# The first sequence's two channel mixing chunks side by side, and the weight conversions spread evenly over attention

## The chip, the cores and the metric

The kernel runs on one core of a Trainium2 chip. The metric is device microseconds of one execution; before the change the median of three runs is 427.49 us (426.55 to 429.01). The profiled execution is one of these runs, and all durations below come from it.

TensorE (PE) multiplies, with its weight loads (PEld) beside it; VectorE (DVE), ScalarE (ACT) and GpSimd (POOL) work on tiles; SP issues nearly all DMAs. Each engine executes its own queue in order.

## The reference, cut to what matters

Three layers follow each other: a linear attention with decay (2 sequences, 8 heads, 768 tokens, head size 48), a mixer, and a mixture of 8 experts in which each token takes one.

```python
# attention, per head:  y_t = r_t (S + u k_t v_t);  S = w S + k_t v_t
# mixer, per sequence, x is [768, 384]:
h  = np.maximum(xt @ w_tok1, 0.0) @ w_tok2        # over tokens, 768 -> 256 -> 768
u  = x + h.transpose(0, 2, 1)
h2 = np.maximum(u @ w_ch1, 0.0) @ w_ch2           # over channels, 384 -> 1536 -> 384
x  = u + h2
# experts: logits and a gate choose e per token
h = np.maximum(x[b, s] @ w1[e], 0.0);  out[b, s] = p[e] * (h @ w2[e])
```

The four mixer weights arrive as float64, everything else as float32.

## The kernel before, in words

Every product of the mixer is done in float32 by three matmuls: both operands are split into a rounded part (hi) and a rest (lo), and hi·hi, lo·hi, hi·lo are added in PSUM (`mm3`, L353). A split is a copy on ACT and a subtraction on DVE or POOL.

**Conversions.** The float64 weights are converted on the chip in 16 items, each half of a weight block: `c1k` and `c2k` are blocks of the channel mixing's first and second product, `t1` and `t2` are the token mixing's. One item takes the absolute value on ACT (`conv_abs`, L294), three DVE parts (`conv_parts`, L314: part A is two instructions, L320 and L321, part B is L325, part C is L327), and then a copy on ACT and a subtraction on POOL (`conv_finish`, L284), which are issued when the next item begins. Part C also issues the load of a later item's raw bits. `conv_do(n)` issues n parts at the place where it is called. The order of all instructions is the order in which the Python code issues them; no scheduler changes it.

**Attention** is a loop over 12 tiles of 128 tokens (t = 0 to 11, six per sequence). Iteration t does for tile t+1 the scores on PE and the masks `am` on DVE, for tile t+2 the scaling of `rk` (`pre_rk`, L369) and the product `pp` on DVE, then the state update, the values `y` of tile t on PE, the `bon` products of tile t+1 on ACT (L391), and `finish(t)` (L479), which forms `x` on DVE, issues a conditional DMA into it (taken only where the decay lies outside a range) and splits `x` into `xh` and `xl`. Transposes (`turn`, and `pre_ks`, which makes `kt` of tile t+2) and the token mixing's products (`mix1`, `mix2`) close the iteration. `CONV_T`, `CONV_N` and the other tables at the top say at which t how many parts are issued: three parts in each of t = 2 to 6 and 8 to 10, two ahead of `finish` and one behind it.

**The tail and the channel mixing.** Behind the loop stand the rest of the token mixing and the first steps of the channel mixing, with two more items among them (`CONV_B`). The channel mixing has four chunks n of 384 tokens, two per sequence, and each runs 12 steps f (`chan_step`, L676). A step is nine matmuls `ch1` into a PSUM tile `c1`, the split of its rectified result into `hh` (ACT) and `hl` (DVE) and, two steps later, nine matmuls `ch2` into three accumulators. The chunks run one after another. Steps f use quarter-blocks in order, so chunk 0 needs two new items for every two steps; the last six items are issued among its steps, one whole item per step. While chunk n+1 runs, chunk n's tokens are routed to experts (`route`, whose `yield`s cut it into ten pieces, two per step from f = 3). `usplit(n)` splits chunk n's input into `uh` and `ul`.

PSUM has eight banks: three accumulators (`acc0` to `acc2`) and five that all other tiles take in turn (`ps_tile`).

Of the kernel before, what the change touches and what calls it, by code (L numbers as in the profile page):

```python
# [30 lines left out]
T1 = 4  # L31
CONV_T = (2, 3, 4, 5, 6, 8, 9, 10)
CONV_B = (1, 1, 1, 1, 1, 1, 0, -1, 0, 0)
ABS_NEXT = (10, 11, 12, 13, 14)
ABS_B = (0, 3)
CONV_N = (0, 0, 2, 2, 2, 2, 2, 2, 2, 2, 2, 0)
HI_MIN, HI_MAX = (float(x) for x in np.array([0x38100000, 0x47EFFFFF], np.int32).view(np.float32))
# [40 lines left out]
def _emit(ctx, tc, a_in, wu, u_row, wt1, wt2, wc1, wc2, wgl, wex, cst_in, cst_a, out):  # L78
# [24 lines left out]

    psw = ctx.enter_context(tc.tile_pool(name="psw", bufs=5, space=PSUM))
    psa = ctx.enter_context(tc.tile_pool(name="psa", bufs=1, space=PSUM))
# [28 lines left out]
    def load_a(t, part=None):  # L134
        if t not in a_t:
            rk = ap.tile([128, 1024], F32, tag="rk", name=f"rk{t}", bufs=4)
            v = ap.tile([128, DM], F32, tag="v", name=f"v{t}", bufs=3)
# [117 lines left out]
    conv = []  # L255
    for k in range(6):
        for h in range(2):
            conv.append((k, h))
    conv += [(k, h) for h in range(2) for k in (6, 7)]
    conv_raw, conv_pend, cpool_, wb2 = [], [], [], []  # L260
    nload = [0]

    def conv_load():
        n = nload[0]
        if n >= len(conv) or (n >= 12 and not cpool_):
# [6 lines left out]
        if n < 12:  # L272
            raw = rawp.tile([128, 768, 2], I32, tag="raw", name="raw")
        else:
            raw = cpool_[0].tile([128, 768, 2], I32, tag=f"e{n - 12}", name="raw")
# [17 lines left out]
    def conv_abs(n):  # L293
# [7 lines left out]
        if wb2:  # L301
            if n < 12:
                late[n % 2] = cpool_[0].tile([128, 1536], I32, tag=f"raw{6 + n % 2}", name="f")
# [10 lines left out]
    def conv_parts():  # L314
        for n in range(len(conv)):
# [19 lines left out]
    tail_at = [-1]  # L335

    def conv_tail(n):
        tail_at[0] += 1
        for j in range(2):
            if ABS_B[j] == tail_at[0]:  # L340
                conv_abs(8 + j)
        if n < 0:
            conv_finish()
        else:
            conv_do(n)
# [174 lines left out]
    def mix2(b, half, c, k=2):  # L520
        w2h, w2l = W["t2"]
        ps = acc_tile(k)
        for m in range(2):
# [9 lines left out]
    def usplit(n):  # L533
        b, half = divmod(n, 2)
        for c in range(3):
            u = xT[b][:, c, half * 384:(half + 1) * 384]
            hi = hp.tile([128, 384], F32R, tag=f"uh{c}", name="uh", bufs=1)
            lo = hp.tile([128, 384], F32R, tag=f"ul{c}", name="ul", bufs=1)
            nc.scalar.copy(hi, u)
            nc.vector.tensor_tensor(out=lo, in0=u, in1=hi.bitcast(F32), op=ALU.subtract)  # L540
            uhl[c] = (hi, lo)

# [25 lines left out]
    for t in range(NT):  # L568
        if t + 3 < NT:
            load_a(t + 3, 0)  # L570
        if t < 2:
            conv_load()
# [30 lines left out]
        if t >= 7:  # L603
# [34 lines left out]

    def ch1(f):
        ch, cl = W[f"c1{f // 4}"]  # L640
        ps = ps_tile("c1", (128, 384))
        for c in range(3):
            o = f % 4 // 2 * 768 + c * 256 + f % 2 * 128
            mm3(ps, ch[:, o:o + 128], cl[:, o:o + 128], *uhl[c], c == 0, c == 2)
        return ps
# [21 lines left out]

    later = []
# [20 lines left out]

    def chan(n, side, then, start=0):  # L690
        for f in range(start, 12):
            chan_step(n, f, side, then)
        for _ in side:
            pass

    conv_tail(CONV_B[0])
    turn(11)
    chan_step(0, 0, nothing, None)
    conv_tail(CONV_B[1])
    mix1(11)  # L700
    conv_tail(CONV_B[2])
    chan_step(0, 1, nothing, None)
    conv_tail(CONV_B[3])
    for half in range(2):
        for c in range(3):
            mix2(1, half, c, (2, 0, 1)[c])
            conv_tail(CONV_B[4 + 3 * half + c])
# [10 lines left out]
    for _ in range(4):  # L718
        conv_load()
# [648 lines left out]
```

## Time and profile before

| what | value |
|---|---|
| median of 3 runs | 427.49 us |
| the profiled execution | 426.55 us |
| its span, first to last instruction | 425.0 us |
| PE busy in the span | 399.2 us (94%) |
| DVE busy | 278.5 us (66%) |
| ACT busy | 192.7 us (45%) |
| POOL busy | 90.0 us (21%) |

The shares are means over stages that differ. Until about 102 us the kernel is in attention, until 117 us in the tail, until 154 us in chunk 0, and chunks 1 to 3 end near 275 us; then the experts follow. The waits say what ended the idle time of an engine, and a group of rows with a shape such as 128x768 names partitions and elements. "Clock" is the share of full speed granted to TensorE.

### The profile page before, as it was taken

Reading aid. Unit: us, or ns where it says so; the run is one execution under the profiler, and the core shown is the slowest. Engines: PE = TensorE matmul, PEld = TensorE weight load, DVE = VectorE, ACT = ScalarE, POOL = GpSimd, SP = SyncE. Lnnn points to the kernel's source line nnn. Section 1 sums busy time; section 2 is a strip of 40 time slices with the busy share of each in tenths; the row PEclk is TensorE's granted clock in tenths of the full one; section 3 lists DMA queues with packets and bytes.
Section 4 is the critical chain, followed back from the end, with each engine's and each line's share of the span. In section 5 each row is a group of like instructions: output and inputs, shape, how many; then the busy total and the mean of one; then the engine's idle time right before and its main releaser. Section 6 shows DMA issues by size and latency. Waiting matters only on the chain. (4 is left out here: it accounts for less than half of the span.)

```text
span 425.0 us, 8637 instructions
## 1 busy us (share of the span) xinstructions
PE 399.2 (94%) x3348; PEld 379.3 (89%) x3348; DVE 278.5 (66%) x592; ACT 192.7 (45%) x459; POOL 90.0 (21%) x83
## 2 busy tenths in 40 slices
PE   7997699997899699999999999999999999999994
PEld 3687597986799599999999999999999999999994
DVE  6669998987979944624361447659677676675431
ACT  2587468683443342112311221642755666654531
POOL 2013444145233310000000001131261132111110
PEclk9898999998999999999999999999999999999998
DMA  7364475323390000100100010881779867662000
GB/s 260 129 210 144 148 256 180 122 89 113 99 349 36 1 2 10 48 0 2 56 2 0 2 56 13 323 300 55 259 285 403 283 220 229 211 209 102 11 31 14
DMA packets 18336, 55.88 MB, mean 131 GB/s; under 512 B 3921, under 2 KB 7795, under 8 KB 18290
## 3 DMA queue, kind: packets, MB, share of 16 engines
q1 hardware_dynamic: 16370, 49.96, 33.9%
q0 software_dynamic: 1920, 5.32, 4.0%
q8 instruction: 27, 0.44, 0.4%
q14 instruction: 19, 0.16, 0.1%
HBM read 52.31 MB, written 5.91 MB: 137 GB/s over the span
## 5 line engine op out<-in xcount | busy, mean ns | idle before, releaser
L1030 DVE TENSOR_TENSOR we<-wr,we 128x768 fp32r<-128x768 f32 x54 | 51.6, 960 | 14.8 <-ACT we L1029 14.8
L359 ACT ACTIVATE hh<-c 128x384 fp32r<-128x384 f32 x48 | 23.4, 490 | 74.4 <-PE c L356 65.7
L360 DVE SCALAR_TENSOR_TENSOR hl<-c,hh 128x384 fp32r<-128x384 f32 x48 | 26.4, 552 | 43.3 <-ACT hh L359 43.3
L356 PE MATMUL acc<-hl,c 128*128 128x384 f32 x144 | 48.6, 337 | 3.5 <-DVE hl L360 3.5
L359 ACT ACTIVATE hh<-e 128x256 fp32r<-128x256 f32 (+1 forms) x72 | 25.2, 350 | 57.3 <-PE e L356 43.4
L360 DVE SCALAR_TENSOR_TENSOR hl<-e,hh 128x256 fp32r<-128x256 f32 (+1 forms) x72 | 27.2, 378 | 35.2 <-ACT hh L359 35.1
L354 PE MATMUL acc<-hh,c 128*128 128x384 f32 x144 | 49.7, 345 | 0.0
L355 PE MATMUL c<-uh,c 128*128 128x384 f32 x144 | 48.5, 337 | 0.6 <-POOL c L288 0.6
L354 PE MATMUL c<-uh,c 128*128 128x384 f32 x144 | 48.5, 337 | 0.0
L356 PE MATMUL c<-ul,c 128*128 128x384 f32 x144 | 48.4, 336 | 0.0
L355 PE MATMUL acc<-hh,c 128*128 128x384 f32 x144 | 48.3, 335 | 0.0
L1029 ACT CAST we<-wr 128x768 fp32r<-128x768 f32 x56 | 46.0, 829 | 2.8 <-DMA wr<-in_wex 2.8
L354 PE MATMUL acc<-we,hh 128*128 128x384 f32 x120 | 42.6, 355 | 0.0
L355 PE MATMUL acc<-we,hl 128*128 128x384 f32 x120 | 40.3, 336 | 0.0
L356 PE MATMUL acc<-we,hh 128*128 128x384 f32 x120 | 40.2, 335 | 0.0
L288 POOL TENSOR_TENSOR c<-f,c 128x768 fp32r<-128x768 f32 x12 | 24.4, 2029 | 45.0 <-ACT c L287 45.0
L356 PEld LDWEIGHTS acc<-hl,c 128*128 128x128 f32 x144 | 27.0, 188 | 4.4 <-DVE hl L360 4.4
L355 PEld LDWEIGHTS c<-uh,c 128*128 128x128 f32 x144 | 27.2, 189 | 1.2 <-POOL c L288 1.2
L354 PEld LDWEIGHTS c<-uh,c 128*128 128x128 f32 x144 | 27.3, 190 | 0.0
L354 PE MATMUL e<-gx,we 128*128 128x256 f32 x96 | 27.3, 284 | 0.0
L356 PEld LDWEIGHTS c<-ul,c 128*128 128x128 f32 x144 | 27.2, 189 | 0.0
L355 PEld LDWEIGHTS acc<-hh,c 128*128 128x128 f32 x144 | 27.1, 188 | 0.0
(228 smaller groups left out, 948.1 us busy)
## 6 DMA issues: line engine op xcount, KB each, us to landing
wr<-in_wex SPq DMA_DIRECT2D x32, 768.0 KB, 7.2
raw<-in_wc SPq DMA_DIRECT2D x12, 768.0 KB, 5.3
rk<-in_a_in SPq DMA_DIRECT2D x12, 512.0 KB, 5.7
raw<-in_wt SPq DMA_DIRECT2D x4, 768.0 KB
v<-in_a_in SPq DMA_DIRECT2D x12, 192.0 KB
x<-yscr SPq DMA_DIRECT2D x12, 192.0 KB
xs<-rows SPq DMA_DIRECT2D x8, 192.0 KB
xs<-row SPq DMA_DIRECT2D x4, 192.0 KB, 3.6
```

Source lines behind the costliest of these rows:

```text
L288: nc.gpsimd.tensor_tensor(out=ls, in0=f, in1=hs.bitcast(F32), op=ALU.subtract)
L354: nc.tensor.matmul(ps, lhsT=lh, rhs=rh, start=first, stop=False)
L355: nc.tensor.matmul(ps, lhsT=ll, rhs=rh, start=False, stop=False)
L356: nc.tensor.matmul(ps, lhsT=lh, rhs=rl, start=False, stop=last)
L359: nc.scalar.activation(out=hi, in_=ps, func=ACTF.Relu)
L360: nc.vector.scalar_tensor_tensor(out=lo, in0=ps, scalar=0.0, in1=hi.bitcast(F32), op0=ALU.max, op1=ALU.subtract)
L1029: nc.scalar.copy(hi[:, cs], raw[:, cs])
L1030: eng.tensor_tensor(out=lo[:, cs], in0=raw[:, cs], in1=hi[:, cs].bitcast(F32), op=ALU.subtract)
```

## The change

1. Chunks 0 and 1 run their steps alternately: chunk 0 does f = 0 to 2 in the tail, then (1,0), (1,1), and then (0,f), (1,f-1) for f = 3 to 11, and (1,11). Eight items are issued among these 21 steps, one part and two parts in turn.
2. For that, chunk 0's accumulators take three of the five shared banks (tags w2 to w4), and the `c1` tiles use the two others (`turn_of`); chunk 1's split input gets tiles of its own, in memory that attention used (`ue`), and is split at the end of the tail.
3. The routing of both chunks moves to chunk 2's steps, with two or three pieces per step from f = 0.
4. In attention two parts are issued in each of t = 1 to 10, all ahead of `finish`, and one at t = 11. The first item's absolute value is taken at t = 0, each later one when the part C ahead of it is issued. One item (three parts) stands in the tail. Items alternate c1 and c2 blocks.
5. `pre_ks(t+2)` moves from the end of iteration t to a place right behind `pre_rk(t+2)`, ahead of the state update and the values. `finish`'s conditional DMA moves from SP to ACT, `v` gets a fourth buffer, and both first raw loads are issued at t = 0.
6. The last `mix2` calls of each sequence use shared banks instead of the accumulators.

```diff
-CONV_T = (2, 3, 4, 5, 6, 8, 9, 10)
-CONV_B = (1, 1, 1, 1, 1, 1, 0, -1, 0, 0)
...
-CONV_N = (0, 0, 2, 2, 2, 2, 2, 2, 2, 2, 2, 0)
+CONV_N = (0, 2, 2, 2, 2, 2, 2, 2, 2, 2, 2, 1)
+CONV_B = (0, 1, 0, 0, 0, 1, 1, -1, 0, 0)
...
+    turn_of, nps = [0, 1, 2, 3, 4], [0]
+
+    def ps_tile(name, shape=(128, 512), k=None):
+        if k is None:
+            k = turn_of[nps[0] % len(turn_of)]
+            nps[0] += 1
+        return psw.tile(list(shape), F32, tag=f"w{k}", name=name)
...
-            if n in ABS_NEXT:
+            if n < len(conv) - 1 and (n < 7 or wb2):
                 conv_abs(n + 1)
...
-        nc.sync.dma_start(out=x, in_=yscr[t], cond=bad > 0, cond_hint=False)
+        nc.scalar.dma_start(out=x, in_=yscr[t], cond=bad > 0, cond_hint=False)
...
         if t + 2 < NT:
             pre_rk(t + 2)
+            if (t + 2) % NCH < NCH - 1:
+                pre_ks(t + 2)
...
-        if t in CONV_T:
-            conv_abs(CONV_T.index(t))
         values(t)
...
-        if t in CONV_T:
+        if t < NT - 1:
             conv_do(CONV_N[t])
-        else:
-            conv_finish()
         finish(t)
-        if t in CONV_T:
-            conv_do(3 - CONV_N[t])
...
-            ch_acc[n] = [acc_tile(c) for c in range(3)]
+            if n == 0:
+                turn_of[:] = [0, 1]
+            ch_acc[n] = [acc_tile(c) if n else ps_tile("acc", (128, 384), 2 + c) for c in range(3)]
...
-    chan_step(0, 1, nothing, None)
+    chan_step(0, 1)
+    chan_step(0, 2)
...
-    conv_abs(10)
+    conv_abs(8)
+    usplit(1)
...
-    later.extend([conv_do] * 10)
-    chan(0, nothing, lambda: usplit(1), 2)
-    chan(1, route(0, None), lambda: usplit(2))
-    chan(2, route(1, None), lambda: usplit(3))
-    chan(3, first(), lambda: None)
+    later.extend([lambda j=j: conv_do(1 + j % 2) for j in range(16)])
+    later.append(conv_do)
+    order = [(1, 0), (1, 1)]
+    for f in range(3, 12):
+        order += [(0, f), (1, f - 1)]
+    order.append((1, 11))
+    side = itertools.chain(route(0, None), route(1, None))
+    done0 = order.index((0, 11))
+    for j, (n, f) in enumerate(order):
+        chan_step(n, f, side, 2 if j >= done0 + 3 else 0)
+    for f in range(12):
+        chan_step(2, f, side, 2 + (f % 3 == 2))
+    for f in range(12):
+        if f == 3:
+            side = itertools.chain(side, first())
+        chan_step(3, f, side, 2)
```

DVE's queue in chunk 0 before: between two rows `hl`, each the split of one step, stands one whole item.

```order
L360 SCALAR_TENSOR_TENSOR hl_1841<-c1_1830,hh_1840 128x384
L320 TENSOR_SCALAR f_1750<-f_1750 128x768
L321 TENSOR_SCALAR f_1750<-f_1750 128x768
L325 SCALAR_TENSOR_TENSOR f_1750<-raw_1754,f_1750 128x768
L327 SCALAR_TENSOR_TENSOR f_1750<-raw_1754,f_1750 128x768
L360 SCALAR_TENSOR_TENSOR hl_1873<-c1_1862,hh_1872 128x384
```

And now, in the alternating steps of chunks 0 and 1:

```order
L358 SCALAR_TENSOR_TENSOR hl_1793<-c1_1782,hh_1792 128x384
L324 TENSOR_SCALAR f_1754<-f_1754 128x768
L325 TENSOR_SCALAR f_1754<-f_1754 128x768
L358 SCALAR_TENSOR_TENSOR hl_1818<-c1_1807,hh_1817 128x384
L329 SCALAR_TENSOR_TENSOR f_1754<-raw_1570,f_1754 128x768
L331 SCALAR_TENSOR_TENSOR f_1754<-raw_1570,f_1754 128x768
L358 SCALAR_TENSOR_TENSOR hl_1847<-c1_1836,hh_1846 128x384
```

One item now spans two steps.

ACT's queue in attention, iteration t = 3 before, from the state rows `st` on: the absolute value (L311) stands ahead of the eight `bon` products.

```order
L473 ACTIVATE st1_187<-kp_645,w128_184 128x96 x4
L311 ACTIVATE f_684<-raw_436 128x768
L388 COPY beta_711<-kp_645 128x8
L391 ACTIVATE bon_713<-v4_434,beta_711 128x48 x8
L287 CAST t1_576<-f_578 128x768
```

And now in t = 2, the first of three iterations (t = 2, 5, 8) whose parts are C of one item and A of the next:

```order
L471 ACTIVATE st0_186<-kp_544,w128_184 128x96 x4
L386 COPY beta_615<-kp_544 128x8
L389 ACTIVATE bon_617<-v3_344,beta_615 128x48 x8
L315 ACTIVATE f_630<-raw_348 128x768
L291 CAST t1_435<-f_437 128x768
```

The absolute value that this iteration's part A reads has moved behind the `bon` products.

PE's queue in attention before: the transposes `kt` of tile 3 stand at the end of iteration t = 1, behind the values `y` and the turn.

```order
L433 MATMUL y_477<-v1_106,am0_364 64x48 x2
L433 MATMUL y_477<-v1_106,am1_366 64x48 x2
L497 MATMUL tp_522<-cta_98,x_419 128x128 x3
L380 MATMUL kt_527<-cta_98,rk3_343 128x128 x4
L444 MATMUL kp_537<-st2_188,cta_98 128x384
```

And now in iteration t = 1:

```order
L401 MATMUL at0_444<-rk2_293 128x128
L401 MATMUL at1_445<-rk2_293 128x128
L378 MATMUL kt_455<-cta_98,rk3_343 128x128 x4
L450 MATMUL kp_442<-uw_180,pp_385 64x2 x8
L459 MATMUL kp_442<-v2_294,ks_371 64x48 x8
L426 MATMUL y_488<-st0_186,rk1_105 64x96 x8
```

The transposes, which read the `rk` that DVE scales in the same iteration, have moved ahead of the update and the values.

## Rows read from the trace of the kernel before

**Rows 1.** The page: busy tenths of PE and DVE in 40 slices.
```profile
PE   7997699997899699999999999999999999999994
DVE  6669998987979944624361447659677676675431
```

**Rows 2.** Windows by stage: length; busy PE, PEld, DVE, ACT, POOL; clock, DMA, GB/s.
```profile
32.23:65.02 32.79, 26.80 (x414) 23.95 (x414) 32.44 (x40) 21.04 (x62) 12.87 (x7) 0.95 0.55 185
65.02:101.62 36.60, 32.68 (x505) 29.02 (x504) 33.50 (x44) 24.93 (x75) 16.43 (x10) 1.00 0.40 128
101.62:117.25 15.63, 14.32 (x70) 13.24 (x70) 11.56 (x18) 6.29 (x12) 4.62 (x5) 0.89 0.33 96
117.25:153.92 36.67, 32.57 (x181) 31.06 (x181) 32.57 (x38) 15.80 (x25) 12.57 (x7) 1.00 0.30 111
153.92:195.00 41.08, 41.08 (x255) 40.53 (x255) 16.85 (x56) 9.01 (x20) 0.93 (x2) 1.00 0.05 15
```

**Rows 3.** Waits of PE: us in total, times, longest.
```profile
PE acc L354 <- DVE xT L529: 3.9, 3, 2.5
PE acc L356 <- DVE hl L360: 3.5, 3, 1.8
...
PE acc L356 <- POOL xl L487: 0.5, 1, 0.5
```

**Rows 4.** Timeline of DVE, one step of chunk 0: start, us, instruction.
```profile
133.29 0.55 DVE L360 SCALAR_TENSOR_TENSOR hl<-c,hh 128x384 fp32r<-128x384 f32 x1
133.76 0.55 DVE L320 TENSOR_SCALAR f<-f 128x768 f32<-128x768 f32 x1
134.41 2.17 DVE L321 TENSOR_SCALAR f<-f 128x768 int32<-128x768 int32 x1
136.61 0.96 DVE L325 SCALAR_TENSOR_TENSOR f<-raw,f 128x768 int32<-128x768 int32 x1
137.60 0.96 DVE L327 SCALAR_TENSOR_TENSOR f<-raw,f 128x768 int32<-128x768 int32 x1
138.48 0.55 DVE L360 SCALAR_TENSOR_TENSOR hl<-c,hh 128x384 fp32r<-128x384 f32 x1
```

**Rows 5.** Timeline of PE: first matmul of two steps that follow each other, chunk 1.
```profile
153.92 0.33 PE L354 MATMUL c<-uh,c 128*128 128x384 f32 x1
...
157.04 0.33 PE L354 MATMUL c<-uh,c 128*128 128x384 f32 x1
```

**Rows 6.** Timeline of DVE in attention, from x of t = 5 to x of t = 6.
```profile
57.05 0.55 DVE L482 TENSOR_TENSOR x<-y,bon 128x384 f32<-128x384 f32 x1
57.52 0.95 DVE L327 SCALAR_TENSOR_TENSOR f<-raw,f 128x768 int32<-128x768 int32 x1
58.38 2.87 DVE L369 TENSOR_TENSOR rk<-rk,PP 128x1024 f32<-128x1024 f32 x1
...
65.02 0.55 DVE L482 TENSOR_TENSOR x<-y,bon 128x384 f32<-128x384 f32 x1
```

**Rows 7.** Timeline of ACT in attention, t = 2 and t = 10.
```profile
29.19 0.94 ACT L311 ACTIVATE f<-raw 128x768 f32<-128x768 f32 x1
...
30.22 1.92 ACT L391 ACTIVATE bon<-v,beta 128x48 f32<-128x48 f32 x8
...
94.92 1.34 ACT L539 CAST uh<-xT 128x384 fp32r<-128x384 f32 x3
```

**Rows 8.** Timeline of DVE, then of POOL, at the end of attention.
```profile
95.52 5.11 DVE L540 TENSOR_TENSOR ul<-xT,uh 128x384 fp32r<-128x384 f32 x3
...
98.09 2.13 POOL L288 TENSOR_TENSOR c<-f,c 128x768 fp32r<-128x768 f32 x1
```

**Rows 9.** Timeline of PE and DVE, route of chunk 0 beside chunk 1's steps.
```profile
170.50 0.16 PE L795 MATMUL cc<-rsb,upb 128*128 128x1 bf16 x1
...
170.89 1.27 DVE L805 TENSOR_SCALAR M<-cb,c 128x384 bf16<-128x384 f32 x3
...
174.08 0.18 DVE L822 CAST ohb<-op 128x24 bf16<-128x24 f32 x1 [0.90 <-PE op L816]
```

More of the change, by code (lines that the diff above doesn't have):

```diff
@@ L1 @@
+import itertools
 from contextlib import ExitStack
@@ L101, in C @@
         return cst[:, a:b]
-    psw = ctx.enter_context(tc.tile_pool(name="psw", bufs=5, space=PSUM))
+    psw = ctx.enter_context(tc.tile_pool(name="psw", bufs=1, space=PSUM))
     psa = ctx.enter_context(tc.tile_pool(name="psa", bufs=1, space=PSUM))
@@ L136, in load_a @@
             rk = ap.tile([128, 1024], F32, tag="rk", name=f"rk{t}", bufs=4)
-            v = ap.tile([128, DM], F32, tag="v", name=f"v{t}", bufs=3)
+            v = ap.tile([128, DM], F32, tag="v", name=f"v{t}", bufs=4)
             a_t[t] = (rk, v)
@@ L255, in _emit @@
     conv = []
[L256 to L259, printed above, removed]
+    for k in range(2):
+        conv += [(k, 0), (k, 1)]
+    for k in range(2, 8, 2):
+        conv += [(k + j, h) for h in range(2) for j in range(2)]
     conv_raw, conv_pend, cpool_, wb2 = [], [], [], []
@@ L264, in conv_load @@
         n = nload[0]
-        if n >= len(conv) or (n >= 12 and not cpool_):
+        if n >= len(conv) or (n >= 10 and not cpool_):
             return
@@ L271, in conv_load @@
             src = (wc1, wc2)[k % 2][(k - 2) // 2]
-        if n < 12:
+        if n < 10:
             raw = rawp.tile([128, 768, 2], I32, tag="raw", name="raw")
         else:
-            raw = cpool_[0].tile([128, 768, 2], I32, tag=f"e{n - 12}", name="raw")
+            raw = cpool_[0].tile([128, 768, 2], I32, tag=f"e{n - 10}", name="raw")
         src = src.bitcast(I32)
@@ L301, in conv_abs @@
         if wb2:
-            if n < 12:
+            if n < 10:
                 late[n % 2] = cpool_[0].tile([128, 1536], I32, tag=f"raw{6 + n % 2}", name="f")
@@ L333, in conv_parts @@
         conv_finish()
-    tail_at = [-1]
     def conv_tail(n):
[L338 to L341, printed above, removed]
         if n < 0:
@@ L521, in mix2 @@
         w2h, w2l = W["t2"]
-        ps = acc_tile(k)
+        ps = acc_tile(k) if k >= 0 else ps_tile("mix", (128, 384))
         for m in range(2):
@@ L536, in usplit @@
             u = xT[b][:, c, half * 384:(half + 1) * 384]
-            hi = hp.tile([128, 384], F32R, tag=f"uh{c}", name="uh", bufs=1)
-            lo = hp.tile([128, 384], F32R, tag=f"ul{c}", name="ul", bufs=1)
+            if n == 1:
+                if c == 0:
+                    six = [cpool_[0].tile([128, 4, 384], F32R, tag=f"e{6 + j}", name="ue") for j in range(2)]
+                hi, lo = six[0][:, c], six[1][:, c]
+            else:
+                hi = hp.tile([128, 384], F32R, tag=f"uh{c}", name="uh", bufs=1)
+                lo = hp.tile([128, 384], F32R, tag=f"ul{c}", name="ul", bufs=1)
             nc.scalar.copy(hi, u)
             nc.vector.tensor_tensor(out=lo, in0=u, in1=hi.bitcast(F32), op=ALU.subtract)
-            uhl[c] = (hi, lo)
+            uhl[n, c] = (hi, lo)
     slow_path(bad)
@@ L570, in _emit @@
             load_a(t + 3, 0)
-        if t < 2:
+        if t == 0:
+            conv_load()
             conv_load()
@@ L595, in _emit @@
             load_a(t + 3, 1)
-        if t in CONV_T:
+        if t < NT - 1:
             conv_do(CONV_N[t])
-        else:
-            conv_finish()
         finish(t)
-        if t in CONV_T:
-            conv_do(3 - CONV_N[t])
+        if t == 0:
+            conv_abs(0)
+        if t == NT - 1:
+            conv_do(CONV_N[t])
         if t >= 7:
@@ L623, in _emit @@
     while m2:
-        mix2(*m2.pop(0))
+        mix2(*m2.pop(0), -1)
     pend = []
@@ L636, in flush, with ch1 @@
             pend.pop(0)()
-    def ch1(f):
+    def ch1(n, f):
         ch, cl = W[f"c1{f // 4}"]
@@ L666, in ch2 @@
                 nc.vector.tensor_tensor(out=u, in0=u, in1=acc[c], op=ALU.add)
+        if n == 0 and f == 11:
+            turn_of[:] = [0, 1, 2, 3, 4]
     later = []
@@ L674, in _emit, with chan_step @@
     nothing = iter(())
-    def chan_step(n, f, side, then):
-        ps = ch1(f)
-        if f >= 3:
+    def chan_step(n, f, side=nothing, nside=0):
+        ps = ch1(n, f)
+        if nside:
             next(side, None)
-        if f == 11:
-            then()
-        if f >= 3:
+        if f == 11 and n in (0, 2):
+            usplit(n // 2 + 2)
+        for _ in range(nside - 1):
             next(side, None)
@@ L688, in chan_step @@
         work()
[L690 to L694, printed above, removed]
     conv_tail(CONV_B[0])
     turn(11)
-    chan_step(0, 0, nothing, None)
+    chan_step(0, 0)
     conv_tail(CONV_B[1])
@@ L705, in _emit @@
         for c in range(3):
-            mix2(1, half, c, (2, 0, 1)[c])
+            mix2(1, half, c, -1 if half else (2, 0, 1)[c])
             conv_tail(CONV_B[4 + 3 * half + c])
@@ L717, in _emit @@
     ident = idw[:, 0, 0:128]
-    for _ in range(4):
+    for _ in range(6):
         conv_load()
@@ L1212, in unit @@
             pass
-    later.extend([conv_do] * 10)
-    chan(0, nothing, lambda: usplit(1), 2)
-    chan(1, route(0, None), lambda: usplit(2))
-    chan(2, route(1, None), lambda: usplit(3))
-    chan(3, first(), lambda: None)
+    later.extend([lambda j=j: conv_do(1 + j % 2) for j in range(16)])
[14 more added lines that the diff above has]
+        chan_step(3, f, side, 2)
+    for _ in side:
+        pass
     flush()
```

8 lines of the change are left out of this document (1 added, 7 removed).

## The prediction

> **What bounds the kernel now.** I read the page's slices first: behind the first slice PE is at 9 tenths except in slices 4, 5, 10, 11 and 14 (and the last) [rows 1]. The reader is to see there that DVE is at 7 to 9 in just these slices and at 1 to 6 in the ten behind them, 15 to 24. So PE bounds the kernel as a whole, and what is left to gain is time in which PE waits for DVE. The windows put sizes on it [rows 2]. From 32 to 65 us (attention, t = 3 to 6) DVE is busy 32.4 of 32.8 us and PE 26.8: DVE bounds. From 65 to 102 us PE is busy 32.7 of 36.6 us: PE bounds, but for 3.9 us. From 102 to 117 us (the tail) the granted clock averages 0.89. From 117 to 154 us (ten steps of chunk 0) DVE is busy 32.6 of 36.7 us, with 181 matmuls. From 154 us on PE is busy all the time up to 195 us and at 9 tenths to the end, and what starts earlier there should end earlier by as much. The list of PE's waits names the causes: `xT` adds on DVE 3.9 us, `hl` on DVE 3.5 us [rows 3].
>
> **Chunk 0's steps.** A step that PE alone paces takes 157.04 - 153.92 = 3.12 us [rows 5]; that is 18 matmuls of 0.173 us from start to start. Ten steps would take 31.2 us; they take 36.67 [rows 2]. DVE sets the pace: one `hl` and one whole item, from `hl` to `hl` 138.48 - 133.29 = 5.19 us [rows 4]. In it L321 takes 2.17 us where the instruction of the same shape ahead of it takes 0.55, because POOL's subtraction of the item before runs beside it; this 1.6 us comes once per item. After the change an item is spread over two steps: 5.19 + 0.47 for the second `hl` (133.76 - 133.29) = 5.66 us of DVE against 2 x 3.12 = 6.24 us of PE. PE should pace these steps, with 0.6 us to spare per pair. Gain: 36.67 - 31.2 = 5.5 us. The bounds: 5.5 us gained if DVE keeps up; and if a second instruction of each item waits for POOL (another 1.6 us, 7.26 us per pair), 21 steps lose (7.26 - 6.24) / 2 = 0.51 us each, 10.7 us in all. I take 5.5, since the row shows one such wait per item.
>
> The two banks left for `c1` should cost nothing: a bank is needed again two steps on, with three groups of nine matmuls (4.7 us) between the end of one `c1` and the start of the next in its bank, and the split needs about 1 us plus at most two parts (1.9 us) ahead of it on DVE [rows 4].
>
> Here a rule speaks against the change. The row first: with PE waiting several times between groups in these steps, 3.5 us in three waits, the clock stayed at 1.00, 2.4 GHz [rows 2, 3]. The Trainium skill (TensorE: Matmul & The Clock Gate, A second HAM failure mode: psum-queue depth-cycling) says that matmul groups that cycle through PSUM banks can leave idle spots often enough for the clock to swing between its two levels. By the row the alternating steps stay at full clock and the sum holds; by the rule some of them would run at 1.2 GHz and lose up to 3.1 us per step, which the rivals price below.
>
> **The end of attention.** At t = 10 DVE's three `ul` instructions last 5.11 us where the ACT copies of the same tiles take 1.34 [rows 7, 8]; POOL's subtractions of two items run beside them, the last from 98.09 us for 2.13 [rows 8]. Behind them on DVE stand `x` of t = 11 and the `xT` add for which PE waits 2.5 us, its longest wait; 0.5 us more is a wait for POOL's `xl` [rows 3]. After this wait the tail runs at a mean clock of 0.89: 0.11 x 15.63 = 1.7 us [rows 2]. In the new order only one item's subtraction falls here (the next one is issued in the tail), and the last token mixing product has a bank of its own, so it waits for no add. I count all of it as gained: 2.5 + 0.5 + 1.7 = 4.7 us. Bounds: 0 if the `ul` rows stay as long, 4.7.
>
> **The DVE-bound part of attention.** Iterations t = 2 to 6 issue two parts instead of three: 5 x 0.95 us [rows 6] = 4.75 us less on DVE, and one item less is finished on POOL, about 1.65 us (in the row `rk` takes 2.87 us for 1024 elements per partition where 768 take 0.95, that is 1.27 by size; the rest, 1.6 us, is the same wait for POOL as L321's [rows 4, 6]). Against it: t = 1 gets two parts; half of them fit where DVE waits for scores, one counts, 0.95 us. And in t = 2 and 5 part A waits for its absolute value, which now stands behind `bon` on ACT: 1.92 + 0.94 us [rows 7], less the part C that DVE does meanwhile, 0.95: 1.9 us each, 3.8 us. (In t = 8 the same wait falls where PE bounds.) Net gain 4.75 + 1.65 - 0.95 - 3.8 = 1.65 us. Bounds: 6.4 us gained if ACT is early, and 2.2 us lost if POOL's locks stay and ACT waits at t = 8 as well (0.95 + 3 x 1.9 - 4.75 = 1.9, and 0.3 for the transposes, below).
>
> Edits that I cost at nothing: the twelve conditional DMAs on ACT stand just ahead of `xh`, which waits for the same `x`; SP's queue gains, since it no longer stands still for `x` ahead of its loads. The two raw loads at t = 0 are issued an iteration or more ahead of the part that needs them. The earlier transposes: behind them on PE stand the state update and the values, and they wait for `rk`, the first instruction of DVE's iteration; where DVE bounds, PE would wait later in the iteration anyway, and where PE bounds, `rk` is early. If that cover is gone, see the slower rival.
>
> **The tail.** Gone: the `xT` waits other than the longest, 3.9 - 2.5 - 0.2 = 1.2 us [rows 3]. New, first: chunk 0's step f = 2 needs the second half of `c10`, whose finish is issued behind step 0's split: a split's ACT copy (half of 0.94), the item's ACT copy (0.94, a row of the same shape) and POOL's subtraction (2.13) make 3.5 us [rows 7, 8]; PE has 15 matmuls in the meantime, 2.6 us. Loss 0.9 us. New, second: chunk 1's input is split into memory that attention used, so ACT starts only when PE has done the last token mixing matmul, and PE's next instruction, `ch1` of (1,0), needs it: the item's absolute value 0.94, one copy 1.34 / 3 = 0.45 [rows 7] and one `ul` of about 0.55 (an `hl`, same shape [rows 4]): 1.9 us in which PE has nothing else. The tail loses 0.9 + 1.9 - 1.2 = 1.6 us. Bounds: 0.7 us (only the absolute value counts and the rest overlaps: 0.94 + 0.9 - 1.2), and 3.3 us, if the clock falls after the wait and costs what it cost before, 1.7 us.
>
> **The routing.** Ten pieces per chunk stay; in the new grouping a DVE piece stands between two PE pieces of one step twice. In one place PE waits from the last `cc` matmul (170.50 + 0.16 = 170.66) to the end of the three `M` (170.89 + 1.27 = 172.16): 1.5 us; in the other for one small copy of 0.18 us and its two hand-overs, about 0.3 us [rows 9]. Loss 1.8 us; bounds 0.3 and 3.0 (the longer one in both places).
>
> **The sum.** -5.5 - 4.7 - 1.65 + 1.6 + 1.8 = -8.45 us. The profiled execution took 426.55 us, so 418.1 us; the median of the runs shown lies 0.94 us above that execution, and the change will be held against it: 427.49 - 8.45 = 419.0 us. The forecast's own range is 416 to 422 us.
>
> **The rivals.**
> 1. Attention gives nothing: the waits for ACT at t = 2, 5, 8 eat the saved parts, and half of the end's 4.7 us stays, because PE's one tile in flight still waits for `x` of t = 11. For it: DVE was the bound there and loses only three parts of 24 in all. Against it: 4.7 us hang on one pile-up of POOL work that the new order does not have. -5.5 - 2.35 + 1.6 + 1.8 = -4.45: 423 us.
> 2. No change that can be measured (within 0.5%, 2.1 us, about what a measurement of this kernel can tell from none): rival 1, and the clock also falls twice, after the wait in front of chunk 1 and after a long wait of PE for the earlier transposes, 1.7 us each. -4.45 + 3.4 = -1.05: 426.4 us. For it: PE's scattered waits in t = 2 to 5 become one long wait per iteration. Against it: of the trace's waits up to 2.5 us only some were followed by a lower clock, and PE is busier than before.
> 3. Slower: DVE stays the pace of the alternating steps. Its place is the pair of steps, its price half of what the pair exceeds 6.24 us, 21 times; it decides from 0.6 us more DVE time per item. With a second POOL lock per item it is 10.7 us: -8.45 + 10.7 = +2.25, 429.7 us. For it: POOL's subtraction now falls beside the next item's part A with an `hl` on either side, and 0.6 us is a thin margin. Against it: the row's lock comes once per item, and POOL has nothing else to do there [rows 4]. The same total would come if the clock swung in some ten of the 21 steps by a third of a step each; the clock of 1.00 in chunk 0 with its waits speaks against that [rows 2].
>
> **How the numbers follow.** Forecast 0.66, rival 1 0.16, rival 2 0.09, rival 3 0.09. Faster by over 0.5% (below 425.35 us) are the forecast and rival 1: 0.82; same 0.09, slower 0.09. The range for 8 in 10 goes from 414.5 us (attention's gain at 6.4 instead of 1.65) to 425.0 us, which takes in rival 1 and leaves out the two others.
>
> **What would show it.** In the profile after: steps of chunks 0 and 1 at 3.12 us from start to start with no waits for `hl`, with part A lengthened once per item; no wait of over 1 us for an `xT` add; `ul` of t = 10 near 3 us; a new wait of PE of about 1.9 us at the first `ue` matmul, and waits of 1.5 us at `op` in chunk 2; in attention A parts that wait for ACT at t = 2 and 5. I am wrong if the pair of steps takes more than 6.3 us, if the first matmul of chunk 0 starts later than 101 us (104.03 before less 3), or if PE idles at half clock inside attention.

## The result, and the profile after

The changed kernel takes 432.82 us (median of 20 runs, 429.69 to 435.84) beside 427.74 us of the kernel before on the same chip (20 runs): a ratio of 1.0139 [1.0112, 1.0166]. It is slower by 1.4%, where 2% faster was forecast (5.1 us more instead of 8.45 us less, a miss of 13.5 us). The profiled execution took 431.78 us, with a span of 430.2. Executions over 1.5% above the fastest of their kernel are left out of the ratios below; of e14's six, four count.

Busy tenths of PE and DVE and the granted clock in 40 slices, and as the last row the clock of the kernel before:

```profile
PE   7895987999989999998989999999999999999994
DVE  6779675478568988537452437568677677675431
PEclk9999789699999999999989999999999999999998
...
PEclk9898999998999999999999999999999999999998
```

PE dips in slices 4, 6 and 7, which are attention, and in 12, 19 and 21; the granted clock falls to 7, 8 and 6 tenths in slices 5, 6 and 8, and to 8 in slice 21, where before it fell to 8 in slices 2, 4 and 10. The windows by stage follow, with the columns of [rows 2]: attention from `x` of t = 2 up to `x` of t = 6 and from there to its end, the tail, the 21 alternating steps, nine steps of chunk 2.

```profile
32.73:63.83 31.10, 24.75 (x352) 22.12 (x353) 25.71 (x34) 17.01 (x53) 12.74 (x7) 0.85 0.41 140
63.83:107.01 43.18, 39.86 (x529) 34.96 (x530) 28.42 (x43) 26.27 (x81) 13.42 (x11) 0.91 0.27 90
107.01:123.67 16.66, 14.45 (x81) 13.49 (x80) 10.43 (x16) 5.64 (x11) 3.95 (x3) 1.00 0.40 125
123.67:189.72 66.05, 66.02 (x378) 65.70 (x379) 47.87 (x60) 23.90 (x41) 15.53 (x8) 1.00 0.21 77
189.72:230.67 40.95, 38.01 (x241) 36.24 (x241) 21.40 (x87) 8.13 (x20) 1.92 (x4) 0.96 0.10 30
```

In [rows 2] DVE was busy 32.4 of 32.8 us up to t = 6 and bounded; now it is busy 25.7 of 31.1 and PE 24.8, so neither bounds: each waits for the other, at a clock of 0.85 where it was 0.95. From x of t = 6 to chunk 0's first matmul it now takes 43.18 us where it took 104.03 - 65.02 = 39.01. The 21 steps run at full clock. PE's waits, as in [rows 3]:

```profile
PE kt L378 <- DVE rk L367: 6.1, 4, 3.0
PE acc L352 <- ACT t L291: 1.5, 1, 1.5
PE c L352 <- ACT ue L542: 1.5, 1, 1.5
...
PE op L818 <- DVE M L807: 1.3, 2, 1.2
...
PE acc L354 <- POOL t L292: 1.0, 1, 1.0
...
PE rkp L845 <- DVE ohb L824: 0.6, 1, 0.6
...
PE c L353 <- POOL c L292: 0.6, 1, 0.6
```

The `xT` waits, and the `hl` waits in chunk 0's steps, are gone. The first row is the earlier transposes, and two rows (1.5 and 1.0 us) are for `t`, the converted token mixing weight. Three stretches are used below; only the first is measured from `x` of t = 0, since the start itself varies by up to 2.5 us between profiles.

| profiled execution | x of t = 0 to chunk 0's first matmul | from there to `tr` of chunk 2's routing | rest of the span |
|---|---|---|---|
| before | 84.8 | 142.9 | 178.1 |
| after | 88.9 | 143.9 | 179.3 |

Attention lost 4.1 us and the middle 1.1, where the terms of the prediction give gains of 5.7 and 2.8 us (of the 1.7 us of clock that it counts at the end of attention, 0.7 lay behind chunk 0's first matmul: a clock of 0.95 over 13.22 us). So the miss is about 10 us in attention and 4 in the middle.

The loss in attention has its place. From `x` of t = 0 to `x` of t = 6 the kernel takes 45.7 us (before: 45.8), so nothing was won there. From there to `x` of t = 10 it takes 36.3 us (before: 28.7), a loss of 7.6 us, and from there to chunk 0's first matmul 6.9 us (before: 10.3), a gain of 3.4.

### The profile page after: what moved, and what is told of

Same layout as the page of the kernel before. It is cut to its first block, busy times and chain, and to the rows that moved or that the text cites. A ratio compares the mean times of both kernels' runs of the same rounds, so it can differ in the third digit from the quotient of the medians.

```text
span 430.2 us, 8623 instructions
## 1 busy us (share of the span) xinstructions
PE 404.6 (94%) x3348; PEld 384.4 (89%) x3348; DVE 273.9 (64%) x592; ACT 192.6 (45%) x459; POOL 89.4 (21%) x83
## 5 line engine op out<-in xcount | busy, mean ns | idle before, releaser
L1032 DVE TENSOR_TENSOR we<-wr,we 128x768 fp32r<-128x768 f32 x54 | 51.6, 960 | 14.8 <-ACT we L1031 14.8
L353 PE MATMUL c<-uh,c 128*128 128x384 f32 x108 | 36.6, 339 | 0.6 <-POOL c L292 0.6
L292 POOL TENSOR_TENSOR c<-f,c 128x768 fp32r<-128x768 f32 x12 | 23.3, 1938 | 66.0 <-ACT c L291 66.0
L352 PE MATMUL c<-uh,c 128*128 128x384 f32 x108 | 36.7, 340 | 0.0
L354 PE MATMUL c<-ul,c 128*128 128x384 f32 x108 | 36.5, 338 | 0.0
L352 PE MATMUL e<-gx,we 128*128 128x256 f32 x96 | 27.2, 284 | 0.0
L353 PEld LDWEIGHTS acc<-hh,c 128*128 128x128 f32 x144 | 27.2, 189 | 0.0
L352 PEld LDWEIGHTS acc<-hh,c 128*128 128x128 f32 x144 | 27.1, 188 | 0.0
L354 PE MATMUL e<-gx,we 128*128 128x256 f32 x96 | 27.0, 281 | 0.0
L353 PE MATMUL e<-gx,we 128*128 128x256 f32 x96 | 27.0, 281 | 0.0
```

The costliest lines, as they stand in the source:

```text
L292: nc.gpsimd.tensor_tensor(out=ls, in0=f, in1=hs.bitcast(F32), op=ALU.subtract)
L352: nc.tensor.matmul(ps, lhsT=lh, rhs=rh, start=first, stop=False)
L353: nc.tensor.matmul(ps, lhsT=ll, rhs=rh, start=False, stop=False)
L354: nc.tensor.matmul(ps, lhsT=lh, rhs=rl, start=False, stop=last)
L1032: eng.tensor_tensor(out=lo[:, cs], in0=raw[:, cs], in1=hi[:, cs].bitcast(F32), op=ALU.subtract)
```

## What the trace shows of attention

DVE in t = 2, from part C of one item to `rk`, the counterpart of [rows 6]; the bracket is the idle time before a row and what ended it:

```profile
27.63 0.95 DVE L331 SCALAR_TENSOR_TENSOR f<-raw,f 128x768 int32<-128x768 int32 x1
31.66 0.56 DVE L324 TENSOR_SCALAR f<-f 128x768 f32<-128x768 f32 x1 [3.08 <-ACT f L315]
32.26 0.56 DVE L325 TENSOR_SCALAR f<-f 128x768 int32<-128x768 int32 x1
32.73 0.55 DVE L480 TENSOR_TENSOR x<-y,bon 128x384 f32<-128x384 f32 x1
33.20 2.38 DVE L367 TENSOR_TENSOR rk<-rk,PP 128x1024 f32<-128x1024 f32 x1
```

Part A waits 3.08 us for its absolute value, which stands behind `bon` on ACT; `x`, long computable, waits behind part A. On PE the iteration t = 4 reads:

```profile
36.24 1.75 PE L401 MATMUL at<-rk 64*128 64x128 f32 x16 [0.62 <-DVE am L413]
40.99 1.08 PE L378 MATMUL kt<-cta,rk 128*128 128x128 f32 x4 [3.00 <-DVE rk L367]
42.01 1.02 PE L450 MATMUL kp<-uw,pp 128*64 128x2 f32 x16
42.88 1.53 PE L426 MATMUL y<-st,rk 128*64 128x96 f32 x16
```

PE has done its scores and stands 3.00 us in front of the transposes, with the update and the values ready behind them. Then it works at half speed (a window's clock stands third from the end):

```profile
36.00:40.00 4.00, 1.64 (x16) 1.26 (x16) 3.97 (x7) 2.22 (x8) 0.45 (x1) 1.00 0.00 0
40.00:44.00 4.00, 3.01 (x34) 2.71 (x36) 3.93 (x7) 2.25 (x8) 1.24 (x1) 0.62 0.89 301
44.00:48.00 4.00, 4.00 (x46) 3.91 (x43) 2.51 (x3) 2.80 (x9) 2.01 (x2) 0.53 0.69 224
...
78.00:82.00 4.00, 4.00 (x15) 2.92 (x16) 1.25 (x2) 0.48 (x1) 0.00 (x0) 0.51 0.00 0
```

The last row is another place, t = 7. There the first token mixing product `mix2` needs the second half of `t2`, whose last part is done in t = 6, but whose finish is issued only when the next item begins, behind the `bon` products of t = 7. PE, then ACT, then POOL:

```profile
74.95 0.60 PE L352 MATMUL acc<-t,t1h 128*128 128x384 f32 x1 [1.55 <-ACT t L291]
...
76.84 0.69 PE L354 MATMUL acc<-t,t1h 128*128 128x384 f32 x1 [0.96 <-POOL t L292]
```
```profile
74.08 0.82 ACT L291 CAST t<-f 128x768 fp32r<-128x768 f32 x1
```
```profile
74.98 1.81 POOL L292 TENSOR_TENSOR t<-f,t 128x768 fp32r<-128x768 f32 x1 [7.54 <-ACT t L291]
```

POOL had idled 7.5 us and ACT could have cast earlier: the place of the finish, not an engine's load, made PE wait. Behind these two waits PE had no other in attention: from 77.32 to 107.01 us it was busy 29.69 of 29.69 us, at a clock of 0.92.

## The experiments

All ratios are to the kernel before, run beside each kernel; the stretches are those of the table above.

| run | ratio | attention | middle |
|---|---|---|---|
| after | 1.0139 [1.0112, 1.0166] | 88.9 | 143.9 |
| e1: `t2` finished in t = 6 | 1.0073 [1.0041, 1.0104] | 84.6 | 143.9 |
| e2: routing regrouped | 1.0022 [0.9992, 1.0051] | 88.2 | 139.3 |
| e3: transposes late | 1.0003 [0.9975, 1.0032] | 84.5 | 144.0 |
| e4: absolute values early | 0.9987 [0.9960, 1.0013] | 84.3 | 143.9 |
| e5: attention as before | 0.9974 [0.9952, 0.9996] | 85.3 | 141.1 |
| e8: e5 + e2 | 0.9916 [0.9885, 0.9946] | 84.0 | 138.1 |
| e6: e1 + e2 + e4 | 0.9893 [0.9858, 0.9927] | 81.9 | 139.4 |
| e7: e6 + e3 | 0.9744 [0.9696, 0.9792] | 78.0 | 140.9 |
| e9: idle matmuls, misplaced | 1.0227 [1.0189, 1.0264] | 88.5 | 143.9 |
| e10: e7, `ue` first | 0.9715 [0.9680, 0.9751] | 74.9 | 138.6 |
| e11: idle matmuls 16, 11 | 1.0113 [1.0089, 1.0137] | 86.6 | 143.9 |
| e12: e6, idle matmuls 16, 16 | 0.9861 [0.9827, 0.9894] | 78.7 | 140.8 |
| e13: idle matmuls 7, 11 | 1.0063 [1.0035, 1.0091] | 90.0 | 143.9 |
| e14: transposes behind `y` | 1.0195 [1.0149, 1.0241] | 92.9 | 144.0 |

**One part undone at a time.** e1:

```diff
             conv_do(CONV_N[t])
+        if t == 6:
+            conv_finish()
         finish(t)
```

> The changed kernel, with one line more: the second half of t2 (the fourth item) is finished at t = 6, right behind its part C, instead of at t = 7 when the next item begins. Theory A (the late finish costs the time in attention: PE waits 1.5 + 1.0 us for it at t = 7, falls to half clock, and x of t = 8 comes 9 us later than before): these two waits go, the low clock at 76 to 82 us goes, and the kernel is 5 to 8 us faster than the changed one, 425 to 428 us. Theory B (the transposes moved ahead of the update, with the waits for rk, cost it): 0 to 2 us, 431 to 433 us, since other low-clock stretches stay and a new one comes.

The waits for `t` went, and the half clock behind them: the same stretch now has this row, where the row of 78 us above had 0.51.

```profile
74.00:82.00 8.00, 8.00 (x121) 7.07 (x120) 5.36 (x8) 4.78 (x19) 1.80 (x1) 1.00 0.30 92
```

0.66 points (1.0139 - 1.0073) is 2.8 us of 427.74: between the two theories, and a loss of its own.

e2, each chunk's routing begins at its own step of chunk 2, two pieces per step:

```diff
-    side = itertools.chain(route(0, None), route(1, None))
+    sides = [route(0, None), route(1, None)]
...
-        chan_step(2, f, side, 2 + (f % 3 == 2))
+        chan_step(2, f, sides[f // 5] if f < 10 else nothing, 2)
```

> The changed kernel, with the routing of both chunks cut into pairs again: chunk 0's ten pieces in steps f = 0 to 4 of chunk 2, two per step, chunk 1's in f = 5 to 9, so that no two pieces with PE work stand in one step. If the three-piece steps cost what the profile shows (waits of 1.2 + 0.65 + 0.5 us and more for M, ohb and hl, and a low clock from 217 to 222 us, 5.7 us between step (2,0) and (2,9) against PE's own need), 3.5 to 5.5 us faster than the changed one, 427 to 429 us. Rival (the routing of two chunks in one chunk is too dense however it is cut: PE's waits for DVE chains stay): 0 to 1.5 us faster, 431 to 433 us.

The waits for `M` and `ohb` went; 1.17 points, 5.0 us (4.6 in the middle stretch of the profile), in the first theory's range.

e3, `pre_ks(t + 2)` back at the end of the iteration:

> The changed kernel, with the transposes kt put back to the end of each iteration. Theory A: the waits of 6.1 us for rk ahead of kt turn into waits at other instructions (scores, update, values), since DVE bounds there; within 1.5 us of the changed kernel, 431.5 to 434 us, and the waits at t = 7 stay. Theory B: the low clock at 40 to 47 and 61 to 65 us goes with the grouped waits, and 3 to 6 us are won, 427 to 430 us.

e4, the absolute value ahead of `bon` in t = 2, 5, 8:

```diff
+        if t in (2, 5, 8):
+            conv_abs({2: 1, 5: 3, 8: 5}[t])
         values(t)
```

> The changed kernel, with the absolute values of items 1, 3 and 5 taken ahead of the bon products in t = 2, 5 and 8, as before the change. DVE's waits for ACT at part A (3.08, 1.78 and 2.76 us) go. If these waits delay x in the DVE-bound iterations and lengthen PE's idle stretch into half clock: 2 to 5 us faster than the changed one, 428 to 431 us. Rival (what is won there is lost in the wait for t2 at t = 7, which then only begins earlier): 0.5 to 2 us faster, 431 to 432.5 us.

1.36 and 1.52 points: 5.8 us in e3, as its theory B had it, and 6.5 us in e4, more than either of its theories had. DVE's wait in t = 2 fell from 3.08 to 1.09 us in e4:

```profile
29.66 0.56 DVE L324 TENSOR_SCALAR f<-f 128x768 f32<-128x768 f32 x1 [1.09 <-ACT f L315]
```

In e4's profile `x` of t = 6 comes 41.9 us behind `x` of t = 0 instead of 45.7, 3.8 us sooner. Each of the two edits alone brings attention back to the time it took before; neither is the cause alone.

**One part alone, and all repairs together.** e5 keeps the chunks, tail and routing of the change and takes attention from before:

> Attention as it was before the change (three parts in each of eight iterations, transposes at the iteration's end, DMA on SP); the tail, the alternating chunks and the routing as in the changed kernel. Theory A (the change of the chunks gains what the prediction gave it, 5.5 us, and only attention and the routing spoil it): the steps gain 5.5, the new wait ahead of chunk 1 takes 0.3 to 2, the routing takes 5.7, so the time is 427.7 + 0.2 to 2.2, 428 to 430 us, and the first matmul of chunk 0 stands near 102 to 104 us. Rival B (the alternating steps also slow the tail or attention's end, by the banks they take): over 431 us, as the changed kernel.

> The same as the run with attention as before, and the routing of each chunk begins at a step of its own with two pieces per step in chunk 2. Theory A (the routing's loss of about 4 us is the grouping of its pieces, wherever attention ends): 4 us below that run, 424 to 426 us. Rival B (the routing's waits hang on how the queues enter chunk 2): within 1 us of it.

> The changed kernel with three repairs at once: the second half of t2 finished at the end of iteration 6, the routing's pieces two per step, and the absolute values of items 1, 3 and 5 ahead of the bon products. Theory A (three separate losses): 432.8 - 2.1 - 4.3 - 4.9 = 421.5 us. Rival B (the first and the third take away the same stretch of half clock, so that only one of them counts): 423.5 us or more, with a granted clock that still falls to 0.50 once or twice between 34 and 80 us.

> The same three repairs, and the transposes kt back at the end of the iteration. Theory A (the transposes cost 5.3 us whatever else is repaired): 416 us. Rival B (late transposes and early absolute values shorten the same waits of PE for DVE in iterations 2 to 5): 420 to 422 us, 1 to 3 us below the run without it.

e5 was better than both theories had it: 1.1 us gained (0.26%), beside 2.1 by the prediction's three terms for these parts. With the routing regrouped (e8) it is 3.6 us: the regrouping gave 2.5 us here, between its two theories, where it gave 5.0 in e2. In e6 the repairs gave less than their sum (0.0246 against 0.0335); the ratio puts its time at 423.2 us, between the two theories, and the clock still fell at 40 and at 66 us, as rival B had it. The transposes then gave 1.49 points more, as much as alone (1.36), as theory A had it. The four repairs together gave 3.95 points, 16.9 us; alone they sum to 4.71. In e7, whose profiled execution was the slowest of its six, attention ends 78.0 us behind `x` of t = 0, 6.8 us earlier than before; forecast was 5.7 for the whole change without repairs.

e10 is e7 with `usplit(1)` ahead of `conv_abs(8)` on ACT.

> The three repairs and the late transposes, and at the end of the tail the split of chunk 1's input ahead of the absolute value of the next item on ACT. Theory A (the absolute value is 0.9 us of the 1.5 us that PE waits for ue, and the wait is what brings the clock down at 116 to 119 us): the wait falls to about 0.6 us, the second group behind it stays at full clock, and the time falls by 0.9 to 2.9 us against the run without it, to a ratio of 0.968 to 0.972. Rival B (the split waits for something else, the last token mixing product): the same wait and a ratio of 0.974 or more.

The first row is that wait in the changed kernel, the other in e10:

```profile
123.67 0.44 PE L352 MATMUL c<-ue,c 128*128 128x384 f32 x1 [1.51 <-ACT ue L542]
```
```profile
108.43 0.45 PE L352 MATMUL c<-ue,c 128*128 128x384 f32 x1 [0.72 <-ACT ue L542]
```

The wait fell by 0.8 us as theory A had it; the ratio, 0.9715, is inside the expected range, but its interval overlaps e7's. It is the best version: 2.9% faster than before. In its profiled execution, the fastest of six, attention ran at full clock, with PE busy 29.3 of 32.8 us up to t = 5 and 41.7 of 42.2 us behind:

```profile
17.66:50.41 32.75, 29.32 (x522) 25.79 (x522) 30.73 (x42) 25.27 (x86) 9.56 (x7) 1.00 0.44 145
50.41:92.57 42.16, 41.72 (x624) 37.59 (x623) 33.65 (x51) 30.24 (x93) 16.69 (x13) 1.00 0.39 128
```

**Clock or order?** Why do earlier transposes cost 5.8 us? Is it the half clock behind PE's long waits, or that the values stand behind these waits? Idle matmuls of zeros ahead of the transposes keep PE at work during its wait (t here is the tile transposed, two ahead of the iteration).

```diff
         kt = ps_tile("kt")
+        for _ in range({6: 16, 8: 11}.get(t, 0)):
+            nc.tensor.matmul(kt[:, 0:384], lhsT=upb[:, 0:128], rhs=upb[:, 0:384], start=True, stop=True)
```

> The changed kernel with idle matmuls of zeros (16 in iteration 3, 11 in iteration 5, 0.16 us each) just ahead of the transposes kt, into the bank that kt then overwrites, so that PE works where it waited 3.0 and 2.0 us for rk. Nothing else moves. Theory A (what the waits for rk cost is mostly the half clock behind them, 41 to 48 and 60 to 66 us): the clock stays at 1.00 there, and the time falls by 3 to 5 us against the changed kernel, to 428 to 430 at a kernel before of 427.7 (ratio about 1.003). Rival B (the cost is the order itself: update and values stand behind the wait, and DVE behind them): the clock stays up and the time falls by under 1.5 us (ratio 1.011 or more).

This one was put at the wrong tiles ({5: 16, 7: 11}), as the next expectation says, and tells nothing of the question.

> The changed kernel with idle matmuls of zeros (16 in iteration 4, 11 in iteration 6, 0.16 us each) just ahead of the transposes kt, where PE waited 3.0 and 2.0 us for rk. The run before put them in iteration 3 and 5: iteration 3 has no transposes and iteration 5 no wait, so it only added 2 us of work. Theory A (what these waits cost is mostly the half clock behind them, 41 to 48 and 61 to 66 us): the clock stays at 1.00 there, and the ratio falls from 1.0139 to 1.002 to 1.007 (3 to 5 us). Rival B (the order itself costs: update and values stand behind the wait): the clock stays up, and the ratio is 1.010 or more.

> The three repairs without the late transposes, and the idle matmuls in iterations 4 and 7 (16 each), where that kernel's PE waited 3.0 and 3.1 us for rk. Theory A: the clock stays at 1.00 to the end of attention, and the ratio comes near that of the run with the late transposes, 0.974 to 0.981. Rival B: the ratio stays near 0.989, that of the run with the three repairs alone.

> The changed kernel with idle matmuls ahead of the transposes kt, 7 in iteration 4 and 11 in iteration 6. The run with 16 in iteration 4 kept the clock at 1.00, but they could start only when the bank of kt came free (1.8 us into the wait), and held kt back by some 1.4 us past rk. With 7 they end about when rk does. Theory A (clock): the ratio falls from 1.0139 to 1.002 to 1.007. Theory B (order): it stays at 1.008 or more, at best 1.4 us (0.003) under the 1.0113 of the run with 16.

> The changed kernel with one move: the transposes kt stand behind the values y of tile t on PE, still ahead of finish, the turn and the token mixing products. Theory B (the loss is that the update and the values stand behind PE's wait for rk): nearly all of the 1.36 points come back that the transposes at the iteration's end gave, a ratio of 1.000 to 1.004. Theory A (any place where PE waits for rk costs the clock): the ratio stays at 1.008 or more, with the clock at 0.50 behind a wait for rk.

In e11's profile the clock stayed at 1.00 where the changed kernel's fell to 0.50:

```profile
40.00:48.00 8.00, 6.23 (x91) 5.03 (x91) 7.33 (x12) 3.97 (x14) 1.24 (x1) 1.00 0.62 201
58.00:66.00 8.00, 7.69 (x103) 6.25 (x101) 6.40 (x7) 5.31 (x18) 3.17 (x2) 1.00 0.47 143
```

Attention took 2.3 us less, against 4.4 with late transposes. The time fell by only 0.26 points, less than the two intervals can tell apart, and 1.0113 is in rival B's range. The idle matmuls' own delay counts in it (in t = 4 `kt` came 3.2 us behind `x` of t = 3, 44.42 - 41.23, where it was 40.99 - 39.16 = 1.8). With seven of them (e13) the time fell by 0.76 points, into theory A's range, but the interval reaches past B's bound of 1.008; its profiled execution, the slowest of nine, had lost the clock ahead of them, so its stretch proves nothing. In e12 attention took 78.7 us, 3.2 less than e6, and so nearly e7's 78.0, but the timed ratio stayed near e6's, as B had it. The times alone leave the question open.

Two pairs of profiles say more. e4 and e6 issue the same instructions up to t = 6, and in both PE waited 3.00 us for `rk` in t = 4. The clock was 0.50 right behind that wait in e4 and 1.00 in e6, where it fell some 2 us later. The first us behind the wait and then `x` of t = 4 on DVE, in e4 and in e6:

```profile
39.25:40.25 1.00, 1.00 (x4) 0.68 (x4) 1.00 (x3) 0.00 (x0) 0.71 (x1) 0.50 0.71 264
44.45 0.56 DVE L480 TENSOR_TENSOR x<-y,bon 128x384 f32<-128x384 f32 x1 [1.50 <-PE y L431]
```
```profile
39.25:40.25 1.00, 0.99 (x19) 0.83 (x20) 1.00 (x3) 0.33 (x1) 0.72 (x1) 1.00 0.80 289
42.95 0.56 DVE L480 TENSOR_TENSOR x<-y,bon 128x384 f32<-128x384 f32 x1
```

In e4 DVE, which bounds here, waits 1.50 us for `y`; in e6 it does not, and `x` comes 5.5 us behind `x` of t = 3, as with late transposes in e3 (44.33 - 38.87). In this place the price is the clock's alone. In e12 and e10, on the other hand, attention ran at a clock of 1.00 throughout:

```profile
19.70:98.40 78.70, 75.46 (x1173) 65.10 (x1173) 63.65 (x92) 55.70 (x177) 26.61 (x20) 1.00 0.39 129
```
```profile
17.66:92.57 74.91, 71.04 (x1144) 63.38 (x1144) 64.38 (x92) 55.51 (x178) 26.25 (x20) 1.00 0.41 136
```

e12, with the early transposes, still takes 3.8 us more. Its idle matmuls held `kt` back by about 1.5 us in t = 4 (42.22, where `rk` was done at 40.71), and in t = 7 not at all, for `kt` still waited 0.3 us for `rk` there; the rest, some 2 us by this estimate, is the order. So both theories hold in part. How the 5.8 us divide between them stays open.

e14 missed theory B's range by far, but by a cause of its own, so it does not decide. Each transpose brings an ACT copy `ks`, and in e14 that copy stands ahead of `bon` in ACT's queue. ACT in t = 2 of e14:

```profile
31.59 0.59 ACT L380 COPY ks<-kt 128x512 f32<-128x512 f32 x1 [1.13 <-PE kt L378]
...
32.28 1.91 ACT L389 ACTIVATE bon<-v,beta 128x48 f32<-128x48 f32 x8
34.10 0.87 ACT L315 ACTIVATE f<-raw 128x768 f32<-128x768 f32 x1
```

ACT idles for `kt`, `bon` and the absolute value come later, DVE's part A waits 3.9 us, and `x` of t = 2 comes 17.3 us behind `x` of t = 0. In the changed kernel it comes 14.6 us behind it and in e3 14.8, so there the transposes cost nothing yet in t = 2. Nor does e14 bear out theory A, though its ratio is in A's range: its two waits of over 2 us, 2.8 for `x` and 2.9 for `t`, were not for `rk`.

## Why the prediction was wrong, point by point

- **Chunk 0's steps: right.** The 21 steps take 66.05 us, the first 3.58 and the others 3.12 each; DVE's rows in one of them, beside [rows 4], carry one long L325 per item. First matmul of the last step and of the next chunk, as [rows 5]:

```profile
139.44 0.55 DVE L324 TENSOR_SCALAR f<-f 128x768 f32<-128x768 f32 x1
140.09 2.02 DVE L325 TENSOR_SCALAR f<-f 128x768 int32<-128x768 int32 x1
142.08 0.56 DVE L358 SCALAR_TENSOR_TENSOR hl<-c,hh 128x384 fp32r<-128x384 f32 x1
```
```profile
186.59 0.33 PE L352 MATMUL c<-ue,c 128*128 128x384 f32 x1
...
189.72 0.33 PE L352 MATMUL c<-uh,c 128*128 128x384 f32 x1
```

  The third rival fell with that. The granted clock was 1.00 over the whole stretch, and PE was busy 66.02 of 66.05 us. The Trainium skill's rule (TensorE: Matmul & The Clock Gate, A second HAM failure mode: psum-queue depth-cycling) starts from idle spots between matmul groups; these steps had none, so the rule had no case here.
- **The end of attention: right, but its gain was covered.** The `ul` rows take 2.48 us (5.11 in [rows 8], "near 3" forecast), the long `xT` wait is gone and the tail's clock is 1.00. From `x` of t = 10 to chunk 0's first matmul 3.4 us were won, where the term gives 4.0 for this stretch. The loss ahead of it hid the gain.
- **The DVE-bound part of attention: a term mis-sized, and this step failed.** It counted the two late absolute values as 1.9 us of DVE each; DVE waited 3.08 us in t = 2 and 1.78 in t = 5. In t = 2 the wait was handed on: `x`, then `rk`, then PE. Up to `x` of t = 6 nothing was won, where 1.65 us were forecast. The third wait, 2.76 us in t = 8, cost PE nothing, as the prediction had it, since PE was busy throughout there. The repair is worth 6.5 us, where the prediction had counted 3.8 as the price. (Its bound of 6.4 leaves out the 0.95 us that it charges for t = 1, and its first reading of [rows 1] is too sharp: DVE is at 7 to 9 in all slices from 4 to 14, also where PE is at 9.)
- **"The earlier transposes cost nothing": failed.** The argument was that PE would wait later in the iteration anyway. But before, PE had the values to do while DVE scaled `rk`; the move turned scattered waits into one of 3.00 us, behind which the clock fell, and DVE then waited 1.49 us for the late values (`x` of t = 4). Rival 2 named this, with one fall for 1.7 us; it is worth 5.8 us. (The 0.3 us for the transposes in the prediction's bound of 2.2 has no derivation.)
- **Not seen at all: when `t2` is due.** The prediction counted parts per iteration and never asked which product needs an item and when its finish is issued. At t = 7 PE waited 2.5 us for it and then worked at half clock until about 82 us; by e1 it is worth 2.8 us.
- **The tail: nearly right.** New waits of 0.6 us for `c10` (0.9 forecast) and 1.51 for `ue` (1.9), as predicted; from chunk 0's first matmul to chunk 1's first the change was +0.3 us (16.66 against 13.22 and one more step of 3.12), where 1.6 less the 0.7 of clock was forecast.
- **The routing: a term mis-sized.** 1.8 us forecast. Ten steps of chunk 2 (189.72 to 233.79) took 5.8 us more than ten steps of 3.12 and twice the 3.5 us by which routing lengthened chunk 1 before (40.99 us for twelve steps, with PE busy throughout). The waits seen (1.3 us for `M`, 0.65 for `ohb`, some 0.8 for `hl`) add up to 2.8, where 1.8 were read from [rows 9]; behind the longest the clock fell for 4 us, 1.7 us lost at its rate, which was not priced; some 1.3 us of the 5.8 I can't place, and e2 keeps as much. PE's row, then the windows:

```profile
216.64 0.18 PE L818 MATMUL op<-oh,M 128*128 128x8 bf16 x1 [1.18 <-DVE M L807]
```
```profile
218.00:220.00 2.00, 2.00 (x9) 2.00 (x8) 1.37 (x10) 0.00 (x0) 0.00 (x0) 0.61 0.00 0
220.00:222.00 2.00, 2.00 (x9) 1.99 (x7) 0.00 (x0) 0.00 (x0) 0.00 (x0) 0.54 0.15 9
```

- **The rivals.** The slower one (429.7 us) had the right sign by the wrong mechanism. Rival 2's two falls of the clock came in part: not behind the wait for `ue`, but behind waits for `rk` and `t2`. Two of the three signs named for a failure came up: chunk 0's first matmul at 107.01 us, past 101, and PE at half clock inside attention.
- **The sum.** The four repairs give back 16.9 us, of which the forecast had counted 5.6 as a price (3.8 for the absolute values, 1.8 for the routing). So they account for 11.3 of the 13.5 us between forecast and result; of the other 2, about 1 is what chunk 0's first step (3.58 instead of 3.12) and the end of attention (3.4 instead of 4.0) fell short of, and the rest has no place.

## What to carry to other kernels

Where work is spread more evenly over a loop, list for each product when it is due and when the last step that makes it (here the cast and subtraction) is issued: fewer parts per iteration finish later. An instruction moved ahead in an in-order queue must be checked for what becomes of the work that used to cover its wait, on every engine it issues to: here the move put PE's values behind a wait, and in e14 ACT's `bon` as well. And where two engines bound in turn, a wait on the one is handed on to the other, and a long one on PE brings the clock down behind it.

## What the runs showed of the hardware that I had not expected

In the sixteen profiles (before, after, e1 to e14) all sixteen waits of PE of 2.0 to 4.2 us between 16 and 128 us were followed by a granted clock of 0.50 (1.2 GHz) within 4 us, for some 3 to 9 us. Shorter waits went either way: the same wait of 1.5 us for `ue` was followed by 0.50 in e3, e4, e7, e11 and e12 and by 1.00 in the nine others that have it. Where the clock fell, the step behind it took 5.0 to 5.1 us (e7: 113.91 to 119.01) instead of 3.5 to 3.6. So a wait that looks like 1.5 us in one profile is worth 1.5 or 3 in another execution. The spread of such a kernel goes with its clock: of e7's six executions the two fastest (412.8 us) had a mean granted clock of 0.997 and 0.998, the two slowest (418.7 and 419.0 us) 0.981 and 0.982.
